# One u tile in eight transposed by TensorE instead of VectorE and DMA, with half of its output product in native fp32, and output copies in pairs

## Chip, cores and metric

The kernel runs on one core of a Trainium2 chip, as one program of 30891 instructions. The metric is the device time in microseconds of one execution. Three runs of the kernel before gave 1365.64, 1365.99 and 1366.42 us; the median is 1365.99 us.

## What is computed

The reference has three parts that follow each other on an array of 8 x 3072 rows with 256 columns: a spectral layer (FFT, complex weights, soft threshold, inverse FFT), a soft mixture of experts with 32 slots, and a feed-forward layer with a normalised softmax. The change touches only the last one, here with N = 24576 rows:

```python
def _moe2_ref(x, w_in, w_out, g_ln):
    h = x @ w_in                                   # N x 1024
    e = np.exp(h - h.max(-1, keepdims=True))
    sm = e / (e.sum(-1, keepdims=True) + 1e-09)
    solu = h * sm
    mu, var = solu.mean(-1), solu.var(-1)
    ln = (solu - mu) / np.sqrt(var + 1e-06) * g_ln
    return ln @ w_out                              # N x 256
```

## The kernel before

Phase 1 (to about 655 us) does the spectral layer and the experts' statistics; phase 2, from there to the end, does all that `_moe2_ref` asks for. Phase 2 works on NI = 192 tiles of 128 rows. The order of its instructions is written out by hand: the loop `for i in range(NI + 6)` at the end of `phase2` calls small functions, each for another tile, and every engine takes its instructions in that order. In iteration i the calls that matter are:

- `hmat(i + 3)`: two TensorE products of 512 columns write h, negated, into a PSUM tile `hps` (pool `ph_p`, 3 buffers). The columns of h stand in the permuted order of `gst`.
- `rowmax(i + 2)`, `umul(i + 1)`, `blocks(i + 1)`: VectorE's three passes of 1024 columns. `umul` multiplies h by its exponential into `u` (SBUF) and is the last reader of `hps`. `blocks` transposes u in blocks of 32 x 32 into `tb`; then four DMAs on SP's queue move the blocks between partitions into `t2` (128 KB each), so that `t2` holds u transposed.
- `store(i - 6)` and `late_c(i)`: further DMAs on SP's queue. An output store of 512 KB goes out every fourth iteration; a reload of the coefficients `ct` (four DMAs of 128 KB) every eighth. Both fall in iterations with i mod 8 = 7.
- `outp(i - 6)`, `vari(i)`, `expo(i + 2)`, `uhi(i - 1)`: ScalarE's passes: output copy from `po` to `osb`, squares for the variance, exponential of h, and the rounding of 768 of the 1024 columns of `t2` to fp32r (`uh`).
- `uhi(i - 1)` and `ulo(i - 1, n)`: on GpSimd the rounding of the other 256 columns and two subtractions that leave the remainder `ul`. `rstd` adds four small instructions every fourth iteration.
- `prod(i - 3)`: 24 fp32r products of 256 columns into `po`: uh by gw_h, uh by gw_l, then ul by gw_h. Two tiles share one PSUM tile `po2` (pool `po_p`, 2 buffers), so that the first product of an even tile waits until both tiles of the pair two back are copied out.

The last two tiles (`direct(i)`) already go another way: TensorE transposes u (`trans`, line 92, with `gstn`, an h in natural column order), and `direct_parts` splits the result.

A few lines that say more than a sentence:

```python
ps = ph_p.tile([128, DFF], F32, name="hps", tag="hps")     # hmat
SP.dma_start(out=t2[:, a, :], in_=t[z].rearrange("i (b x) -> i b x", b=4))   # blocks, a = 0..3
mm(ps, uh[:, f, :], gw[:, f, 0, :], f == 0, False)         # prod, f = 0..7
mm(ps, uh[:, f, :], gw[:, f, 1, :], False, False)
mm(ps, ul[:, f, :], gw[:, f, 0, :], False, f == 7)         # prod, second loop
```

Of the kernel before, what the change touches and what calls it, by code (L numbers as in the profile page):

```python
# [8 lines left out]
F32 = mybir.dt.float32  # L9
F32R = mybir.dt.float32r  # L10
# [3 lines left out]
AF = mybir.ActivationFunctionType  # L14
ALU = mybir.AluOpType
# [20 lines left out]
def kernel(  # L36
# [24 lines left out]
    PE, ACT, DVE, POOL, SP = nc.tensor, nc.scalar, nc.vector, nc.gpsimd, nc.sync  # L61
    B, N, D = x.shape
# [5 lines left out]
    DFF = 1024  # L68
    NI = T // 128
# [775 lines left out]
    def phase2(p2: ExitStack, pw: ExitStack):  # L845
        k_p = p2.enter_context(tc.tile_pool(name="k2_p", bufs=1))
        c_p = p2.enter_context(tc.tile_pool(name="c_p", bufs=1))

        gw = k_p.tile([128, 8, 2, D], F32R, name="gw")
        gw_h, gw_l = gw[:, :, 0, :], gw[:, :, 1, :]  # L850
        gst = k_p.tile([128, DFF], F32R, name="gst")
        gstn = k_p.tile([128, DFF], F32R, name="gstn")
        cts = {}


# [8 lines left out]
        p = ExitStack()  # L864
# [5 lines left out]
        ps = pt.tile([128, 2, 32], F32, name="pslt", tag="pt")  # L870
# [62 lines left out]
        v = psl.rearrange("p d (o s) -> p d o s", o=1).to_broadcast([128, 2, 4, 32])  # L933
# [3 lines left out]
        for fh in range(2):  # L937
            n = 0
# [13 lines left out]
        def right(name, bufs, **k):  # L952
            return p2.enter_context(tc.tile_pool(name=name, bufs=bufs, side="right", **k))

        e_p = right("e_p", 2)
        u_p = right("u_p", 4)
        o_p = right("o_p", 2)
# [3 lines left out]
        po_p = right("po_p", 2, space=PSUM)  # L961
        NG = NI // 4
        ctt, hps, et, ut, uht, stt, osb, pot = {}, {}, {}, {}, {}, {}, {}, {}


        def pieces(j):
            if j >= NG:
                return
            b, r = divmod(j, 6)
            h, ah = divmod(r, 2)  # L970
            src = cts[b, h][:, 16 * ah:16 * ah + 16, :].rearrange("p a j -> p (a j)")
            ctt[j] = src
            if ah:
                c_todo[4 * j + 3] = (b + 1, h)


        def hmat(i):
            if i >= NI:
                return
            j, k = divmod(i, 4)  # L980
            ps = ph_p.tile([128, DFF], F32, name="hps", tag="hps")
            for fh in range(2):
                mm(ps[:, 512 * fh:512 * fh + 512], ctt[j][:, 128 * k:128 * k + 128], (gstn if direct(i) else gst)[:, 512 * fh:512 * fh + 512])
            hps[i] = ps

        def stats(i):
            j, k = divmod(i, 4)
            if k == 0 and j not in stt:
                stt[j] = s_p.tile([128, 6, 4], F32, name="st", tag="st")
            return stt[j], k  # L990

        def rowmax(i):
            if i >= NI:
                return
            st, k = stats(i)
            DVE.tensor_reduce(out=st[:, 0, k:k + 1], in_=hps[i], op=ALU.min, axis=AX.X)  # L996

        def expo(i):
            if i >= NI:
                return  # L1000
            st, k = stats(i)
            e = e_p.tile([128, DFF], F32, name="e", tag="e")
            ACT.activation(out=e, in_=hps[i], func=AF.Exp, bias=st[:, 0, k:k + 1], scale=-1.0, accum_out=st[:, 1, k:k + 1])  # L1003
            et[i] = e

        def umul(i):
            if i >= NI:
                return
            st, k = stats(i)
            u = u_p.tile([128, DFF], F32, name="u", tag="u")  # L1010
            DVE.scalar_tensor_tensor(out=u, in0=hps.pop(i), scalar=1.0, in1=et.pop(i), op0=ALU.mult, op1=ALU.mult, accum_out=st[:, 2, k:k + 1])  # L1011
            ut[i] = u


        def direct(i):
            return i >= NI - 2

        def gst_order():
            POOL.tensor_copy(out=gstn.rearrange("p (c j b) -> p b c j", c=8, b=4), in_=gst.rearrange("p (b c j) -> p b c j", b=4, c=8).bitcast(F32))

        def blocks(i):
            if i >= NI or direct(i):
                return
            t = u_p.tile([128, DFF], F32, name="tb", tag="tb", bufs=3)
            DVE.transpose(out=t, in_=ut[i])  # L1027
            t2 = u_p.tile([128, 4, 256], F32, name="t2", tag="t2", bufs=3)
            for a in range(4):
                z = slice(32 * a, 32 * a + 32)  # L1030
                SP.dma_start(out=t2[:, a, :], in_=t[z].rearrange("i (b x) -> i b x", b=4))  # L1031
            t2t[i] = t2
# [9 lines left out]
        def parts(i):  # L1042
            uh = u_p.tile([128, 8, 128], F32R, name="uh", tag="uh")
            ul = u_p.tile([128, 8, 128], F32R, name="ul", tag="ul")
            uht[i] = (uh, ul)
            return uh, ul
# [9 lines left out]
                DVE.tensor_tensor(out=ul[:, z, :], in0=ps[:, z, :], in1=uh[:, z, :].bitcast(F32), op=ALU.subtract)  # L1056


        HA = 6

        def uhi(i):
            if i < 0 or direct(i):
                return
            uh, ul = parts(i)
            v = t2t[i].rearrange("p a (c j) -> p c a j", c=8)
            w = uh.rearrange("p c (a j) -> p c a j", a=4)
            ACT.activation(out=w[:, 0:HA], in_=v[:, 0:HA], func=AF.Copy)  # L1067
            POOL.tensor_copy(out=w[:, HA:8], in_=v[:, HA:8])  # L1068

        def ulo(i, n):  # L1070
            if i < 0 or direct(i):
                return
            uh, ul = uht[i]
            z = slice(4 * n, 4 * n + 4)
            v = t2t[i].rearrange("p a (c j) -> p c a j", c=8)[:, z]
            w = uh[:, z, :].rearrange("p c (a j) -> p c a j", a=4)
            POOL.tensor_tensor(out=ul[:, z, :].rearrange("p c (a j) -> p c a j", a=4), in0=v, in1=w.bitcast(F32), op=ALU.subtract)  # L1077
            if n:
                t2t.pop(i)


        def vari(i):
            if i >= NI:
                return
            st, k = stats(i)
            sq = e_p.tile([128, DFF], F32, name="sq", tag="sq", bufs=1)
            ACT.activation(out=sq, in_=ut.pop(i), func=AF.Square, bias=st[:, 2, k:k + 1], scale=-float(DFF), accum_out=st[:, 3, k:k + 1])  # L1087

        def prod(i):
            if i < 0 or i >= NI:  # L1090
                return
            uh, ul = uht.pop(i)
            if i % 2 == 0:
                pot[i // 2, 0] = po_p.tile([128, 2, D], F32, name="po2", tag="po2")
            ps = pot[i // 2, 0][:, i % 2, :]
            for f in range(8):
                mm(ps, uh[:, f, :], gw[:, f, 0, :], f == 0, False)
                mm(ps, uh[:, f, :], gw[:, f, 1, :], False, False)
            for f in range(8):
                mm(ps, ul[:, f, :], gw[:, f, 0, :], False, f == 7)  # L1100
            pot[i] = ps


        def rstd(i):
# [9 lines left out]
            POOL.tensor_tensor(out=st[:, 3, k], in0=st[:, 3, k], in1=st[:, 1, k], op=ALU.add)  # L1114
            POOL.tensor_tensor(out=st[:, 4, k], in0=st[:, 3, k], in1=mhalf[:, k], op=ALU.pow)

        o_todo = {}

        def outp(i):
            if i < 0:  # L1120
                return
            j, k = divmod(i, 4)
            b, r = divmod(j, 6)
            h, ah = divmod(r, 2)
            v = out.rearrange("(b h lm a) d -> b h lm a d", b=B, h=3, a=8)[b, h, :, 4 * ah:4 * ah + 4, :]
            if k == 0:
                osb[0] = o_p.tile([128, 4, D], F32, name="osb", tag="osb")
            o = osb[0]
            ACT.activation(out=o[:, k], in_=pot.pop(i), func=AF.Copy, scale=stt[j][:, 4, k:k + 1])  # L1129
            if j == NG - 1:  # L1130

                SP.dma_start(out=v[:, k, :], in_=o[:, k, :])
            elif k == 3:
                o_todo[i + 2] = (v, o)


        def store(i):
# [36 lines left out]
        expo(1)  # L1174
        umul(0)
        blocks(0)
        for i in range(NI + 6):
            j, k = divmod(i, 4)
            hmat(i + 3)
            trans(i)  # L1180
            rowmax(i + 2)
            umul(i + 1)
            blocks(i + 1)
            store(i - 6)
            late_c(i)
            last_c(i)
            outp(i - 6)
            vari(i)
            expo(i + 2)
            direct_parts(i)  # L1190
            if i <= NI:
                uhi(i - 1)
                ulo(i - 1, 0)
            rstd(i)
            if i <= NI:
                ulo(i - 1, 1)
            if i == 40:
                gst_order()
            if k == 1:
                pieces(j + 2)  # L1200
            prod(i - 3)
        while o_todo:
            store(min(o_todo))
# [140 lines left out]
```

## Time and profile before

| | |
|---|---|
| median of three runs | 1365.99 us |
| profiled execution: span from first to last instruction | 1364.4 us (the page gives no other time for it; the median lies 1.6 us above) |
| busy share of the span: PE, DVE, ACT, POOL | 93%, 88%, 76%, 72% |
| phase 2, from tile 50 to tile 191 (836.9 to 1342.4 us): busy us of 505.5 | PE 476.3, DVE 492.8, ACT 472.9, POOL 461.6 |

PE is TensorE, DVE VectorE, ACT ScalarE, POOL GpSimd, and SPq SyncE's queue of DMA issues. The shares over the whole span mix two phases with different limits; the windows of phase 2 are the ones to read. An instruction's recorded duration overlaps that of its successor on the same engine, so the cost of one is read from its start to the next one's start.

### The profile page before, as it was taken

To read this page: it belongs to the slowest core of one execution; us is meant where nothing else is said; L and a number is where in the kernel's file an instruction comes from. 1 tells how busy PE (TensorE), PEld (TensorE's weight loads), DVE (VectorE), ACT (ScalarE), POOL (GpSimd) and SP (SyncE) were. 2 spreads that over 40 slices of the span, in tenths; PEclk is the share of its full clock that TensorE was granted. 3 is DMA by queue.
4 is the path that set the end of the run, shared out by engine and by line. 5 is a ranking of instruction groups with operands and counts; after the bars stand their busy time and mean duration, and the time that the engine had idled before them with its cause. 6 is when DMAs were issued, how large, how long until landed. Compare 5 with 4: busy or idle time off the path is not lost.

```text
span 1364.4 us, 30891 instructions
## 1 busy us (share of the span) xinstructions
PE 1268.9 (93%) x10784; PEld 1126.9 (83%) x10784; DVE 1207.1 (88%) x1691; ACT 1038.8 (76%) x2005; POOL 979.4 (72%) x1045
## 2 busy tenths in 40 slices
PE   6999999999999999878699989999999999899998
PEld 3888888888878788855588888988898889888897
DVE  7787988888888989765999999999999999999994
ACT  5567665666667665533799889999899999899995
POOL 5557575757565654221588989989899999889996
PEclk8899999999999999999799999999999999999999
DMA  8966463646445464168478788778877888787874
GB/s 267 289 202 175 124 193 111 209 117 186 140 144 167 126 181 155 62 223 291 108 179 220 188 210 209 198 197 209 205 194 203 196 198 217 196 206 191 201 197 125
DMA packets 190746, 252.70 MB, mean 185 GB/s; under 512 B 21504, under 2 KB 155392, under 8 KB 190592
## 3 DMA queue, kind: packets, MB, share of 16 engines
q1 hardware_dynamic: 190256, 249.57, 67.3%
q8 instruction: 85, 1.39, 0.4%
q10 hardware_dynamic: 336, 1.18, 0.2%
q14 instruction: 69, 0.57, 0.1%
HBM read 91.94 MB, written 59.11 MB: 111 GB/s over the span
## 4 chain that ended last, share of the span: by engine, by line
PE 37%; POOL 14%; DMA 13%; issue 12%; DVE 10%; SPq 8%; ACT 6%; POOLq 0%; ACTq 0%; DVEq 0%
PE po L89 10%; DMA t<-tb 9%; POOL ul L1077 8%; PE pb L89 6%; PE pm L89 6%; SPq L1031 6%; PE s L89 4%; PE xps L89 4%; PE pa L89 3%; DMA xc<-in_x_dram 3%; POOL x L235 2%; PE sps L92 2%; SPq L861 2%; POOL uh L1068 2%; ACT uh L1067 1%
## 5 line engine op out<-in xcount | busy, mean ns | idle before, releaser
L1077 POOL TENSOR_TENSOR ul<-t,uh 128x512 fp32r<-128x512 f32 x380 | 486.1, 1296 | 31.8 <-ACT uh L1067 30.7
L89 PEld LDWEIGHTS po<-gw,uh 128*128 128x128 f32 x3072 | 384.9, 190 | 80.8 <-ACT osb L1129 72.2
L89 PE MATMUL po<-gw,uh 128*128 128x256 f32 x3072 | 404.9, 284 | 41.7 <-ACT osb L1129 41.4
L346 POOL TENSOR_TENSOR s<-yb,s 128x512 f32<-128x512 f32 x95 | 132.4, 1394 | 216.9 <-DVE s L345 187.8
L1027 DVE STREAM_TRANSPOSE tb<-u 128x1024 f32<-128x1024 f32 x190 | 236.7, 1246 | 7.0 <-DMA t<-tb 0.4
L1011 DVE SCALAR_TENSOR_TENSOR u<-hps,e 128x1024 f32<-128x1024 f32 x192 | 232.3, 1210 | 11.6 <-ACT e L1003 11.1
L996 DVE TENSOR_REDUCE st<-hps 128x1 f32<-128x1024 f32 x192 | 227.7, 1186 | 1.7 <-PE hps L89 1.7
L1087 ACT ACTIVATE sq<-u,st 128x1024 f32<-128x1024 f32 x192 | 221.3, 1152 | 0.2 <-DVE u L1011 0.2
L1003 ACT ACTIVATE e<-hps,st 128x1024 f32<-128x1024 f32 x192 | 214.1, 1115 | 7.2 <-DVE st L996 6.6
L89 PE MATMUL po<-gw,ul 128*128 128x256 f32 x1536 | 213.0, 281 | 0.8 <-POOL ul L1077 0.8
L89 PEld LDWEIGHTS po<-gw,ul 128*128 128x128 f32 x1536 | 195.3, 189 | 1.1 <-POOL ul L1077 1.0
L1067 ACT ACTIVATE uh<-t 128x768 fp32r<-128x768 f32 x190 | 160.5, 845 | 44.6 <-DMA t<-tb 41.1
L235 POOL TENSOR_TENSOR x<-xc,x 96x512 fp32r<-96x512 f32 x120 | 164.7, 1381 | 29.5 <-ACT x L234 28.4
L89 PE MATMUL hps<-gst,ct 128*128 128x512 f32 x380 | 119.5, 397 | 12.0 <-DVE u L1011 10.5
L261 ACT ACTIVATE asb<-s 96x512 f32<-96x512 f32 x112 | 66.6, 595 | 73.8 <-PE s L89 73.2
L89 PE MATMUL s<-x,df_h 96*96 96x512 f32 x240 | 105.0, 440 | 12.9 <-ACT x L234 4.6
L1068 POOL CAST uh<-t 128x256 fp32r<-128x256 f32 x190 | 75.9, 400 | 49.9 <-DMA t<-tb 46.3
L89 PEld LDWEIGHTS xps<-d_sb,apt 128*128 128x128 f32 x768 | 99.4, 194 | 14.1 <-issue 2.9
L89 PE MATMUL xps<-d_sb,apt 128*128 128x128 f32 x768 | 105.8, 281 | 2.1 <-DMA apt<-ad 1.6
L1129 ACT ACTIVATE osb<-po,st 128x256 f32<-128x256 f32 x192 | 89.5, 468 | 10.2 <-PE po L89 9.1
L234 ACT ACTIVATE x<-xc 96x512 fp32r<-96x512 f32 x120 | 75.1, 626 | 13.2 <-DMA xc<-in_x_dram 13.2
L297 DVE TENSOR_TENSOR xsum<-xps,xi 128x256 f32<-128x256 f32 x96 | 39.8, 414 | 47.9 <-ACT xh L296 44.8
(204 smaller groups left out, 2232.1 us busy)
## 6 DMA issues: line engine op xcount, KB each, us to landing
t<-tb SPq DMA_DIRECT2D x760, 128.0 KB, 2.8
apt<-ad SPq DMA_DIRECT2D x96, 256.0 KB, 4.2
out_dram<-osb SPq DMA_DIRECT2D x47, 512.0 KB, 3.7
xc<-in_x_dram SPq DMA_DIRECT2D x56, 384.0 KB, 3.9
ad<-asb SPq DMA_DIRECT2D x56, 384.0 KB, 3.4
ct<-c_dram SPq DMA_DIRECT2D x96, 128.0 KB, 3.9
wt<-in_moe_w_dram SPq DMA_DIRECT2D x21, 512.0 KB, 8.8
ws<-in_moe_w_dram SPq DMA_DIRECT2D x22, 256.0 KB, 5.9
```

Of the source, the lines that this page charges most:

```text
L89: PE.matmul(out=out, lhsT=lhsT, rhs=rhs, start=start, stop=stop)
L235: POOL.tensor_tensor(out=lo, in0=t, in1=hi.bitcast(F32), op=ALU.subtract)
L346: (DVE if last else POOL).tensor_tensor(out=s, in0=y, in1=s, op=ALU.subtract)
L996: DVE.tensor_reduce(out=st[:, 0, k:k + 1], in_=hps[i], op=ALU.min, axis=AX.X)
L1003: ACT.activation(out=e, in_=hps[i], func=AF.Exp, bias=st[:, 0, k:k + 1], scale=-1.0, accum_out=st[:, 1, k:k + 1])
L1011: DVE.scalar_tensor_tensor(out=u, in0=hps.pop(i), scalar=1.0, in1=et.pop(i), op0=ALU.mult, op1=ALU.mult, accum_out=st[:, 2, k:k + 1])
L1027: DVE.transpose(out=t, in_=ut[i])
L1067: ACT.activation(out=w[:, 0:HA], in_=v[:, 0:HA], func=AF.Copy)
L1068: POOL.tensor_copy(out=w[:, HA:8], in_=v[:, HA:8])
L1077: POOL.tensor_tensor(out=ul[:, z, :].rearrange("p c (a j) -> p c a j", a=4), in0=v, in1=w.bitcast(F32), op=ALU.subtract)
L1087: ACT.activation(out=sq, in_=ut.pop(i), func=AF.Square, bias=st[:, 2, k:k + 1], scale=-float(DFF), accum_out=st[:, 3, k:k + 1])
L1129: ACT.activation(out=o[:, k], in_=pot.pop(i), func=AF.Copy, scale=stt[j][:, 4, k:k + 1])
```

## The change

For tiles with i mod 8 = 5 between 16 and 190 (21, 29, ..., 189: 22 tiles, `turned(i)`) VectorE's block transpose and the four DMAs fall away. In iteration i - 1, after 16 of the 24 products of another tile, TensorE transposes u (8 instructions) back into the tile's own `hps` buffer; ScalarE copies all 1024 columns to SBUF (`raw`); GpSimd splits only columns 512 to 1023 into a high and a low part. The tile's output product has 4 products in native fp32 for the first half (with `gwf`, the sum of gw's two parts) and 12 in fp32r for the second. Its h is made with `gstn`. In iteration i the product of tile i - 3 is split around `hmat(i + 3)`, and `expo` goes ahead of `vari`. Output copies are made two at a time in every even iteration; a store now follows its copy by the same two iterations, and so falls in iterations with i mod 4 = 2. `gst_order` moves from i = 40 to i = 8, and four sums make `gwf` in iterations 10 to 16.

```diff
+        f_p = right("f_p", 1)
+        gwf = f_p.tile([128, 8, D], F32, name="gwf")
+        gstn = f_p.tile([128, DFF], F32R, name="gstn")
...
-                mm(ps[:, 512 * fh:512 * fh + 512], ctt[j][:, 128 * k:128 * k + 128], (gstn if direct(i) else gst)[:, 512 * fh:512 * fh + 512])
+                mm(ps[:, 512 * fh:512 * fh + 512], ctt[j][:, 128 * k:128 * k + 128], (gstn if direct(i) or turned(i) else gst)[:, 512 * fh:512 * fh + 512])
...
+        def turned(i):
+            return i % 8 == 5 and 16 < i < NI - 2
...
+        def gw_sum(n):
+            z = slice(2 * n, 2 * n + 2)
+            POOL.tensor_tensor(out=gwf[:, z], in0=gw[:, z, 0].bitcast(F32), in1=gw[:, z, 1].bitcast(F32), op=ALU.add)
+
         def blocks(i):
-            if i >= NI or direct(i):
+            if i >= NI or direct(i) or turned(i):
                 return
...
+        def turn(i):
+            ps = hps.pop(i).rearrange("p (c j) -> p c j", c=8)
+            for c in range(8):
+                tp(ps[:, c, :], ut[i][:, 128 * c:128 * c + 128])
+            raw, hl = parts(i)
+            ACT.activation(out=raw.bitcast(F32), in_=ps, func=AF.Copy)
+
+        def turned_parts(i, n):
+            raw, hl = uht[i]
+            r = raw[:, 4:8].bitcast(F32)
+            if n == 0:
+                POOL.tensor_copy(out=hl[:, 0:4], in_=r)
+            else:
+                POOL.tensor_tensor(out=hl[:, 4:8], in0=r, in1=hl[:, 0:4].bitcast(F32), op=ALU.subtract)
...
-        def prod(i):
+        def prod(i, left=0):
...
+                if turned(i):
+                    ops = [(uh[:, f, :].bitcast(F32), gwf[:, f, :]) for f in range(4)]
+                    hi = [(f, ul[:, f - 4, :], ul[:, f, :]) for f in range(4, 8)]
+                else:
+                    ops = []
+                    hi = [(f, uh[:, f, :], ul[:, f, :]) for f in range(8)]
+                for f, h, _ in hi:
+                    ops += [(h, gw[:, f, 0, :]), (h, gw[:, f, 1, :])]
+                ops += [(l, gw[:, f, 0, :]) for f, _, l in hi]
...
+            ops = pr_ops[i]
+            while len(ops) > left:
+                mm(*ops.pop(0))
...
-                o_todo[i + 2] = (v, o)
+                o_todo[i + 1] = (v, o)
...
-        for i in range(NI + 6):
+        for i in range(NI + 5):
             j, k = divmod(i, 4)
+            if turned(i):
+                prod(i - 3, 12)
             hmat(i + 3)
...
-            outp(i - 6)
-            vari(i)
-            expo(i + 2)
+            if i % 2 == 0:
+                outp(i - 6)
+                outp(i - 5)
+            if turned(i):
+                expo(i + 2)
+                vari(i)
+            else:
+                vari(i)
+                expo(i + 2)
...
-            if i == 40:
+            if i == 8:
                 gst_order()
+            if i in (10, 12, 14, 16):
+                gw_sum(i // 2 - 5)
...
+            if turned(i + 1):
+                prod(i - 3, 8)
+                turn(i + 1)
             prod(i - 3)
```

TensorE before, iteration 20 and the one behind it (`po` is the output product, of tiles 17 and 18, `hps` the h of the tile three ahead):

```order
L89 MATMUL hps<-gst,ct 128x512 x2
L89 MATMUL po_9957<-gw,uh 128x256 x16
L89 MATMUL po_9957<-gw,ul 128x256 x8
L89 MATMUL hps<-gst,ct 128x512 x2
L89 MATMUL po_10057<-gw,uh 128x256 x16
```

TensorE after the change, the same place: iteration 20, iteration 21 and the start of 22. Line 92 is the transposes of tile 21, into its own `hps` buffer:

```order
L89 MATMUL hps<-gst,ct 128x512 x2
L89 MATMUL po_9966<-gw,uh 128x256 x16
L92 MATMUL hps<-ident,u 128x128 x8
L89 MATMUL po_9966<-gw,ul 128x256 x8
L89 MATMUL po_10047<-gw,uh 128x256 x12
L89 MATMUL hps<-gst,ct 128x512 x2
L89 MATMUL po_10047<-gw,uh 128x256 x4
L89 MATMUL po_10047<-gw,ul 128x256 x8
L89 MATMUL hps<-gst,ct 128x512 x2
```

Eight transposes now stand between the 16th and the 17th product of tile 17, and the next h stands behind 8 and 12 products (of tiles 17 and 18) that follow the transposes, where 24 products stood between one h and the next.

ScalarE after the change, iteration 20 to the start of 22 (line 1169 is the output copy, 1118 `vari`, 1005 `expo`, 1094 `uhi`, 1073 the copy of the transposed tile 21):

```order
L1169 ACTIVATE osb<-po_9862,st 128x256 x2
L1118 ACTIVATE sq,st<-u,st 128x1024
L1005 ACTIVATE e,st<-hps,st 128x1024
L1094 ACTIVATE uh<-t_9896 128x768
L1073 ACTIVATE uh<-hps 128x1024
L1005 ACTIVATE e,st<-hps,st 128x1024
L1118 ACTIVATE sq,st<-u,st 128x1024
L1094 ACTIVATE uh<-t_9947 128x768
L1169 ACTIVATE osb<-po_9966,st 128x256 x2
```

Before, each iteration had one output copy, then `vari`, `expo` and `uhi`. Now iteration 20 has two output copies and, behind `uhi`, the copy of tile 21; iteration 21 has none of these and begins with `expo`.

SP's queue before, the blocks of tiles with i mod 8 = 0 to 5 (line 1031), with the store (1140) and the reload of `ct` (861):

```order
L1031 DMA t_11372<-tb 128x1x256 x4
L1140 DMA out_dram<-osb 128x1024
L861 DMA ct<-c_dram 32x1024 x4
L1031 DMA t_11431<-tb 128x1x256 x4
L1031 DMA t_11479<-tb 128x1x256 x4
L1031 DMA t_11529<-tb 128x1x256 x4
L1031 DMA t_11578<-tb 128x1x256 x4
L1140 DMA out_dram<-osb 128x1024
L1031 DMA t_11632<-tb 128x1x256 x4
```

SP's queue after the change, tiles with i mod 8 = 3, 4, 6, 7, 0 and 1 (blocks line 1040, store 1180, reload 860):

```order
L1040 DMA t_11505<-tb 128x1x256 x4
L1180 DMA out_dram<-osb 128x1024
L1040 DMA t_11556<-tb 128x1x256 x4
L1040 DMA t_11674<-tb 128x1x256 x4
L1040 DMA t_11710<-tb 128x1x256 x4
L1180 DMA out_dram<-osb 128x1024
L1040 DMA t_11757<-tb 128x1x256 x4
L860 DMA ct<-c_dram 32x1024 x4
L1040 DMA t_11814<-tb 128x1x256 x4
```

Store and reload now have a tile's blocks between them, and four DMAs are gone between the blocks of tiles 4 and 6.

## Rows read from the trace of the kernel before

**Rows 1.** Windows by stage: busy us (x instructions) of each engine, granted clock, DMA share.
```profile
0.00:655.00 655.00, 614.23 (x5782) 513.59 (x5782) 534.92 (x924) 393.36 (x854) 347.44 (x262) 0.98 0.57 175
836.90:1342.40 505.50, 476.28 (x3663) 446.66 (x3663) 492.82 (x563) 472.91 (x847) 461.58 (x564) 1.00 0.81 201
```

**Rows 2.** Timeline, DVE: `umul` of tiles 2, 26, 50 and 191 (start us, us).
```profile
661.39 1.21 DVE L1011 SCALAR_TENSOR_TENSOR u<-hps,e 128x1024 f32<-128x1024 f32 x1
...
746.24 1.21 DVE L1011 SCALAR_TENSOR_TENSOR u<-hps,e 128x1024 f32<-128x1024 f32 x1
...
836.88 1.21 DVE L1011 SCALAR_TENSOR_TENSOR u<-hps,e 128x1024 f32<-128x1024 f32 x1
...
1342.42 1.23 DVE L1011 SCALAR_TENSOR_TENSOR u<-hps,e 128x1024 f32<-128x1024 f32 x1 [0.88 <-ACT e L1003]
```

**Rows 3.** Timeline, DVE: one tile's three passes and the next tile's first.
```profile
1117.11 1.19 DVE L996 TENSOR_REDUCE st<-hps 128x1 f32<-128x1024 f32 x1
1118.21 1.21 DVE L1011 SCALAR_TENSOR_TENSOR u<-hps,e 128x1024 f32<-128x1024 f32 x1
...
1119.47 1.25 DVE L1027 STREAM_TRANSPOSE tb<-u 128x1024 f32<-128x1024 f32 x1
1120.64 1.19 DVE L996 TENSOR_REDUCE st<-hps 128x1 f32<-128x1024 f32 x1
```

**Rows 4.** Timeline, PE: one iteration from h to h (xcount: that many in a row).
```profile
1121.78 0.63 PE L89 MATMUL hps<-gst,ct 128*128 128x512 f32 x2
1122.24 2.04 PE L89 MATMUL po<-gw,uh 128*128 128x256 f32 x16
1124.12 1.10 PE L89 MATMUL po<-gw,ul 128*128 128x256 f32 x8
1125.06 0.62 PE L89 MATMUL hps<-gst,ct 128*128 128x512 f32 x2
```

**Rows 5.** Timeline, ACT: one iteration from output copy to output copy.
```profile
1118.35 0.46 ACT L1129 ACTIVATE osb<-po,st 128x256 f32<-128x256 f32 x1
...
1119.84 1.10 ACT L1003 ACTIVATE e<-hps,st 128x1024 f32<-128x1024 f32 x1
1120.84 0.19 ACT L1003 ACTIVATION_READ_ACCUMULATOR e<-hps,st 128x1 f32 x1
1120.92 0.84 ACT L1067 ACTIVATE uh<-t 128x768 fp32r<-128x768 f32 x1
1121.66 0.46 ACT L1129 ACTIVATE osb<-po,st 128x256 f32<-128x256 f32 x1
```

**Rows 6.** Timeline, POOL: `rstd`, then one tile's rounding and subtractions.
```profile
715.05 0.19 POOL L1112 TENSOR_SCALAR st<-st 128x4 f32<-128x4 f32 x1
...
716.86 1.29 POOL L1077 TENSOR_TENSOR ul<-t,uh 128x512 fp32r<-128x512 f32 x1
718.09 0.40 POOL L1068 CAST uh<-t 128x256 fp32r<-128x256 f32 x1
718.45 2.55 POOL L1077 TENSOR_TENSOR ul<-t,uh 128x512 fp32r<-128x512 f32 x2
720.95 0.39 POOL L1068 CAST uh<-t 128x256 fp32r<-128x256 f32 x1
```

**Rows 7.** Waits, 700 to 1350 us: who waits for whom (us in total, times, longest).
```profile
PE po L89 <- ACT osb L1129: 40.7, 40, 2.3
ACT uh L1067 <- DMA t<-tb: 40.7, 38, 2.4
...
DVE u L1011 <- ACT e L1003: 10.9, 19, 1.1
```

**Rows 8.** Timeline, ACT: `uhi` behind store and reload, and behind a store alone [idle before].
```profile
1161.33 0.84 ACT L1067 ACTIVATE uh<-t 128x768 fp32r<-128x768 f32 x1 [2.13 <-DMA t<-tb]
...
1176.00 0.84 ACT L1067 ACTIVATE uh<-t 128x768 fp32r<-128x768 f32 x1 [1.27 <-DMA t<-tb]
```

**Rows 9.** Timeline, PE: the transposes of tile 190 and what follows; then their window.
```profile
1343.14 1.03 PE L92 MATMUL pu<-ident,u 128*128 128x128 f32 x8
1343.93 2.15 PE L89 MATMUL po<-gw,uh 128*128 128x256 f32 x16
...
1343.00:1344.00 1.00, 1.00 (x12) 1.00 (x10) 0.65 (x2) 1.00 (x3) 0.84 (x3) 1.00 0.93 192
```

**Rows 10.** Timeline, PE: native fp32 products of 256 columns (two and a half of them).
```profile
603.25 1.24 PE L89 MATMUL pgm<-wo,ones 128*128 128x256 f32 x5
```

**Rows 11.** Lines by form, 700 to 1350 us: busy us, mean ns of one.
```profile
L92 PE MATMUL pu<-ident,u 128*128 128x128 f32 x16 | 2.1, 272 | 0.0
...
L1019 POOL CAST gstn<-gst 128x1024 fp32r<-128x1024 f32 x1 | 2.1, 2059 | 0.0
```

More of the change, by code (lines that the diff above doesn't have):

```diff
@@ L851, in phase2 @@
         gst = k_p.tile([128, DFF], F32R, name="gst")
-        gstn = k_p.tile([128, DFF], F32R, name="gstn")
         cts = {}
@@ L1010, in umul @@
             u = u_p.tile([128, DFF], F32, name="u", tag="u")
-            DVE.scalar_tensor_tensor(out=u, in0=hps.pop(i), scalar=1.0, in1=et.pop(i), op0=ALU.mult, op1=ALU.mult, accum_out=st[:, 2, k:k + 1])
+            DVE.scalar_tensor_tensor(out=u, in0=hps[i] if turned(i) else hps.pop(i), scalar=1.0, in1=et.pop(i), op0=ALU.mult, op1=ALU.mult, accum_out=st[:, 2, k:k + 1])
             ut[i] = u
@@ L1062, in uhi @@
             if i < 0 or direct(i):
+                return
+            if turned(i):
+                turned_parts(i, 0)
                 return
@@ L1071, in ulo @@
             if i < 0 or direct(i):
+                return
+            if turned(i):
+                if n:
+                    turned_parts(i, 1)
                 return
@@ L1087, in vari @@
             ACT.activation(out=sq, in_=ut.pop(i), func=AF.Square, bias=st[:, 2, k:k + 1], scale=-float(DFF), accum_out=st[:, 3, k:k + 1])
-        def prod(i):
+        def prod(i, left=0):
             if i < 0 or i >= NI:
                 return
[L1092 to L1101, printed above, removed]
+            if i not in pr_ops:
+                uh, ul = uht.pop(i)
+                if i % 2 == 0:
+                    pot[i // 2, 0] = po_p.tile([128, 2, D], F32, name="po2", tag="po2")
+                ps = pot[i // 2, 0][:, i % 2, :]
+                if turned(i):
[7 more added lines that the diff above has]
+                ops += [(l, gw[:, f, 0, :]) for f, _, l in hi]
+                pot[i] = ps
+                pr_ops[i] = [(ps, a, b, n == 0, n == len(ops) - 1) for n, (a, b) in enumerate(ops)]
+            ops = pr_ops[i]
+            while len(ops) > left:
+                mm(*ops.pop(0))
         def rstd(i):
@@ L1115, in rstd @@
             POOL.tensor_tensor(out=st[:, 4, k], in0=st[:, 3, k], in1=mhalf[:, k], op=ALU.pow)
-        o_todo = {}
+        o_todo, pr_ops = {}, {}
         def outp(i):
-            if i < 0:
+            if i < 0 or i >= NI:
                 return
@@ L1176, in phase2 @@
         blocks(0)
-        for i in range(NI + 6):
+        for i in range(NI + 5):
             j, k = divmod(i, 4)
+            if turned(i):
+                prod(i - 3, 12)
             hmat(i + 3)
@@ L1186, in phase2 @@
             last_c(i)
-            outp(i - 6)
-            vari(i)
-            expo(i + 2)
+            if i % 2 == 0:
+                outp(i - 6)
+                outp(i - 5)
+            if turned(i):
+                expo(i + 2)
[3 more added lines that the diff above has]
+                expo(i + 2)
             direct_parts(i)
```

## The prediction

> **What bounds the kernel now.** I read the windows by stage first, to see whether one engine fills a stage: phase 1 is not touched by the change, and in phase 2 between tiles 50 and 191 all four engines are busy for 91 to 97% of 505.5 us, VectorE most [rows 1]. With shares so close, busy time does not tell the bound, so I went to the timelines and read each engine's cost of one tile from start to start.
>
> VectorE takes 3.53 us per tile (1117.11 to 1120.64), of which the block transpose is 1.17 (1119.47 to 1120.64) [rows 3]. TensorE takes 3.28 us (1121.78 to 1125.06): h 0.46, 16 products 1.88, 8 products 0.94 [rows 4]. ScalarE takes 3.31 us (1118.35 to 1121.66), with 0.74 for `uhi` [rows 5]. GpSimd takes 2.86 us (718.09 to 720.95), and `rstd` 1.81 more every fourth tile (715.05 to 716.86) [rows 6]. For eight tiles, the period of the change: VectorE 28.3, GpSimd 8 x 2.86 + 2 x 1.81 = 26.5, ScalarE 26.5, TensorE 26.2.
>
> The real pace is read from `umul`, which every tile has once [rows 2]. Tiles 2 to 26 take 84.85 us for 24 tiles, 28.3 for eight: VectorE alone, without a gap. Tiles 26 to 50 take 90.64 us, 30.2 for eight; in this stretch lie the late work on the last `ct` and `gst_order`. Tiles 50 to 191 take 505.54 us for 141 tiles, 28.7 for eight: VectorE's 28.3 and 0.4 of gaps. Where the gaps come from is in the list of waits: VectorE waits for ScalarE's `e` (10.9 us in total), and ScalarE for the block DMAs (40.7 us, 38 times) [rows 7]. The long ones are behind a store with a reload (2.13 us) and behind a store alone (1.27 us) [rows 8]. So VectorE is the bound, and late DMAs cost a little on top of it.
>
> **The change, part by part, for a group of eight tiles.**
>
> *VectorE.* One transpose goes: 28.3 - 1.17 = 27.1 us. Nothing is added.
>
> *TensorE.* Eight transposes are added. The same eight for tile 190 take 0.79 us, start to the next product's start (1343.14 to 1343.93), at a granted clock of 1.00, the 2.4 GHz level [rows 9]. The turned tile's product loses 12 fp32r products of 1.88 / 16 = 0.118 us each, 1.41 us, and gets 4 native ones. No such product stands in phase 2; the nearest rows are those of the mean of `wo`, same shape, recorded as two instructions for one product. Five of them take 1.24 us, and with 0.16 for the last one's tail (1.10 - 0.94 in [rows 4]) that is 0.216 each, 0.43 per product [rows 10]. Four cost 1.73, so 0.32 more. Sum: 26.2 + 0.79 + 0.32 = 27.3 us. TensorE, now 2 us below VectorE, becomes the highest by 0.2. The bounds of the part it adds: 0.79 + 0 if the native products cost no more than those they replace, and 2.18 + 0.32 if the transposes do not overlap each other, for one alone is recorded with 272 ns [rows 11]. I take 1.1, since [rows 9] is this very instruction in this very place, between products.
>
> *ScalarE.* `uhi` (0.74) goes for the turned tile, and a copy of 1024 PSUM columns comes. The nearest row is `expo`, which reads as many from the same PSUM tile: 1.00 us from its start to its accumulator read [rows 5]. So 26.5 + 0.26 = 26.7 us. Making the output copies two at a time adds none.
>
> *GpSimd.* The turned tile has one cast of 512 columns (between twice the 256-column cast, 0.36 x 2, and half of the 1024-column one, 1.03 [rows 6, 11]) and one subtraction (1.27) in place of 2.86: some 0.7 us less in each group, 25.8. Once, in iterations 10 to 16, four sums of 512 columns are added, which I price as the 512-column subtraction, 4 x 1.27 = 5.1 us, and `gst_order` (2.06 us [rows 11]) comes into the same stretch. GpSimd has 28.3 - 26.5 = 1.8 us of room per group there. Up to tile 26 that is 5 us of room for 7.2 us of work, so I charge 2 us; the bounds are 0 and 7.
>
> *SP's queue and the DMAs.* 22 times four DMAs go. Store and reload no longer stand in one iteration: the blocks behind them now follow one store, or one reload, and the store with i mod 8 = 2 is followed by one tile's blocks and then by a gap of four DMAs. ScalarE comes to those blocks (tile 4) late, because iteration 4 holds two output copies and the turned copy: 4.7 us in place of 3.3. I expect the wait behind the lone store to vanish and the other to shrink, but the period shrinks as well, by about 1 us per group, and leaves less time for each transfer. I count no gain here, and keep the 0.4 us of gaps.
>
> *The PE wait for output copies* (40.7 us, 40 times [rows 7]) goes, for the pair that an even tile needs is now copied one iteration earlier. Today it costs nothing, since VectorE ends last; it is needed so that TensorE, with 27.3 us, can run through.
>
> *The new wait.* The h three tiles ahead needs the turned tile's PSUM buffer, so it waits for `umul`, eight transposes and ScalarE's copy. Let T be the end of `umul` of the turned tile. The transposes end at T + 0.8 at the soonest, the copy at T + 1.9 to 2.2. VectorE asks for that h one full iteration later, at T + 3.5, and h takes 0.46: there are 0.9 to 1.2 us of room. On TensorE 0.94 + 1.41 = 2.35 us of products lie between transposes and h, about twice the copy; behind the h wait the rest of that product and everything after it. If the cover fails, each us by which the copy ends after T + 3.0 costs a us of VectorE, once per group.
>
> **Sum.** The new pace is the highest engine, 27.3, with the gaps of today: 27.7 to 27.8 us for eight tiles, 0.95 below 28.7. Tiles 50 to 191: 141 / 8 x 0.95 = 16.7 us. Tiles 26 to 50, three groups: 3 x 0.95 = 2.8 us. Tiles 2 to 26 have one turned tile: 0.95 gained, 2 charged for GpSimd, -1.0. The end is as before: the last `umul` is followed by the same copies and products. Together 18.5 us off the span of 1364.4, so 1345.9; the median of the runs lies 1.6 us above that span, which gives **1347.5 us**. With the upper TensorE bound in place of 0.79 + 0.32 the gain would be near nothing; with no gaps left (27.3) it would be 1.4 per group and, with the excess of tiles 26 to 50 gone too, some 30 us.
>
> **Rivals.**
>
> *Transposes that do not overlap.* If each of the eight waits for its own weights and its own drain, they cost 8 x 0.272 = 2.18 us [rows 11], TensorE needs 28.7 us per group and is the bound at today's pace: 1366 us, or 1373 us if the 0.4 us of gaps come on top. Against it: 0.79 us for eight [rows 9]. Chance 4%. The Trainium skill (TensorE: Matmul & The Clock Gate, Part 4) gives about 275 ns for a transpose in a kernel and says that transposes do not count as activity for the clock gate. By its figure eight cost 2.2 us, and this change would gain nothing; in [rows 9] the eight took 0.79 us and the granted clock of that stretch stayed at 1.00, so here the trace speaks against both halves of that rule.
>
> *ScalarE and DMA hold the pace.* ScalarE's 26.7 us plus today's DMA waits of 40.7 us over some 180 tiles, 1.8 per group, is 28.5 us. For: the waits of [rows 8] are as long as two transposes. Against: a part of them is room that ScalarE only has because VectorE is slower, and store and reload are now apart. Half-way, at 28.2 to 28.4, the gain is 0.4 per group, 8 us, less 1: 1359 us. Chance 13%.
>
> *The copy comes late (slower).* ScalarE's copy stands behind two output copies, `vari`, `expo` and `uhi`, and that `uhi` can wait 2.13 us for its blocks [rows 8]. If it did so in each group, with ScalarE already 1 us behind, the copy would end near T + 5.3, VectorE would lose 2.3 us where it saves 1.17, and 22 groups would add 25 us: 1391 us. It decides for slower from a copy that ends after T + 4.2. Against: the blocks that this `uhi` needs (tile 3) are issued ahead of the store, not behind it. Chance 8%.
>
> *The change does not do what it says.* The order shows the transposes, the native products (4 with `gwf`) and 22 block transposes fewer. What it does not show is whether the native products run as two passes; if as one, TensorE needs 26.2 + 0.79 - 0.55 = 26.4 and VectorE's 27.1 is the bound: 0.2 per group better, 1344 us. Chance 3%.
>
> **How the numbers follow.** The forecast has 72%. Its own range is 27.3 to 28.1 us per group, 1336 to 1354 us. The range to hold the time 8 times in 10 reaches on to the half-way case: 1336 to 1360 us; left out are the copy that comes late, transposes that do not overlap, and a little at each end. A measurement of this kernel tells about 0.2%, 2.7 us, from no change. Faster by more: 72 + 3 and most of 13, 85%. Within: the no-gain end of two rivals, 6%. Slower: 9%.
>
> **What would show it.** VectorE with 22 transposes fewer and `umul` to `umul` 2.36 us apart once in eight; the eight transposes in 0.8 us at a granted clock of 1.00; the native products at 0.43 us; the copy about 1.0 us; the PE wait for output copies near zero; eight tiles in 27.7 us behind tile 50. I am wrong if PE waits for line 1073 by over 1 us in a group, if VectorE's `rowmax` waits for h, if ScalarE's DMA waits grow, or if tiles 8 to 26 lose more than 2 us to GpSimd.

## The result and the profile after

The change takes 1346.39 us (median of four runs, 1345.94 to 1346.88) against 1366.2 us before, the median of four with a fourth run of 1368.51: the quotient of the two medians is 0.9855. The ratio on record, which the percentages below go by, is 0.9839, 95% interval 0.9822 to 0.9856. The forecast was 1347.5 us, with a range of 1336 to 1360. The span of the profiled execution fell from 1364.4 to 1344.4 us, by 20.0 where 18.5 had been forecast. The number came out right; two terms behind it did not, and they cancelled, so that it came out within 1.1 us is in part luck.

First the windows of the changed kernel, with the columns of [rows 1], for tiles 50 to 191:

```profile
835.50:1322.60 487.10, 485.54 (x3728) 467.65 (x3727) 471.70 (x545) 473.44 (x844) 443.45 (x545) 1.00 0.74 189
```

TensorE is now busy for 485.54 of 487.10 us, VectorE for 471.70, which is 97%; in [rows 1] it was 476.3 and 492.8 of 505.5. TensorE is the fuller engine, as forecast, and its records show next to no gap, where the forecast had kept 0.4 us in each group. Records of TensorE run past the start of the next one, so a short wait can hide in them; one of 0.1 us is read below.

The timeline of VectorE, `umul` of tiles 2, 26, 50 and 191, answers to [rows 2]:

```profile
661.69 1.21 DVE L1013 SCALAR_TENSOR_TENSOR u<-hps,e 128x1024 f32<-128x1024 f32 x1
...
748.63 1.21 DVE L1013 SCALAR_TENSOR_TENSOR u<-hps,e 128x1024 f32<-128x1024 f32 x1
...
835.49 1.21 DVE L1013 SCALAR_TENSOR_TENSOR u<-hps,e 128x1024 f32<-128x1024 f32 x1
...
1322.61 1.22 DVE L1013 SCALAR_TENSOR_TENSOR u<-hps,e 128x1024 f32<-128x1024 f32 x1 [1.11 <-ACT e L1005]
```

| stretch | before, us | after, us | forecast change | measured change |
|---|---|---|---|---|
| tiles 2 to 26 | 84.85 | 86.94 | +1.0 | +2.1 |
| tiles 26 to 50 | 90.64 | 86.86 | -2.8 | -3.8 |
| tiles 50 to 191 | 505.54 | 487.12 | -16.7 | -18.4 |

The rest, -0.2 on the tail and +0.3 ahead of tile 2, makes the 20.0. Behind tile 50 eight tiles take 27.6 us in place of 28.7.

One group of that stretch, the timeline of TensorE (start us, us), from one h to the h of the same place eight tiles on:

```profile
1029.39 0.62 PE L89 MATMUL hps<-gst,ct 128*128 128x512 f32 x2
...
1039.71 2.04 PE L89 MATMUL po<-gw,uh 128*128 128x256 f32 x16
1041.69 1.09 PE L92 MATMUL hps<-ident,u 128*128 128x128 f32 x8
1042.53 1.18 PE L89 MATMUL po<-gw,ul 128*128 128x256 f32 x8
1043.55 1.57 PE L89 MATMUL po<-gw,uh 128*128 128x256 f32 x12
1044.96 0.63 PE L89 MATMUL hps<-gst,ct 128*128 128x512 f32 x2
...
1053.88 1.89 PE L89 MATMUL po<-gwf,uh 128*128 128x256 f32 x8
1055.42 1.78 PE L89 MATMUL po<-gw,ul 128*128 128x256 f32 x12
1057.04 0.62 PE L89 MATMUL hps<-gst,ct 128*128 128x512 f32 x2
```

From 1029.39 to 1057.04 are 27.65 us, and no row shows idle time. The eight transposes take 0.84 us (0.79 in [rows 9]), at a granted clock of 1.00 in that window, the 2.4 GHz level; the turned tile's product 3.16 us (1053.88 to 1057.04), against 3.14 forecast.

The same place on VectorE and ScalarE, with `umul` of the turned tile first (the READ rows are VectorE's accumulator reads, line 1073 the copy of the transposed tile):

```profile
1040.41 1.21 DVE L1013 SCALAR_TENSOR_TENSOR u<-hps,e 128x1024 f32<-128x1024 f32 x1
1041.55 0.08 DVE L1013 DVE_READ_ACCUMULATOR u<-hps,e 128x1 f32 x1
1041.55 1.22 DVE L998 TENSOR_REDUCE st<-hps 128x1 f32<-128x1024 f32 x1
...
1045.70 1.22 DVE L998 TENSOR_REDUCE st<-hps 128x1 f32<-128x1024 f32 x1 [0.51 <-PE hps L89]
```

```profile
1043.01 1.01 ACT L1073 ACTIVATE uh<-hps 128x1024 f32<-128x1024 f32 x1
1043.91 1.10 ACT L1005 ACTIVATE e<-hps,st 128x1024 f32<-128x1024 f32 x1
```

`umul` ends at 1041.63; the transposes start at 1041.69, and the products ahead of them had stretched to 1.98 us from 1.88: TensorE stands at the transposes and waits for u for 0.1 us. The copy is done at about 1043.9, 2.3 us after `umul`, and h starts only at 1044.96, because 20 products stand before it. So `rowmax` waits 0.51 us for h; such a wait stands 14 times in the list below, which covers 22 groups. Two streams close a loop here: VectorE from that `rowmax` to the next turned tile's `umul` end, 27.65 - 4.07 = 23.58 us without a gap, then TensorE from there over transposes, 20 products and h to `rowmax`, 4.07 us (1041.63 to 1045.70).

The list of waits, 700 to 1330 us, answers to [rows 7]:

```profile
ACT uh L1094 <- DMA t<-tb: 19.4, 27, 2.0
DVE u L1013 <- ACT e L1005: 12.1, 17, 1.3
DVE st L998 <- PE hps L89: 7.2, 14, 0.5
```

ScalarE's waits for the block DMAs are half of what they were (40.7), the PE wait for output copies (40.7) has left the list, and the new one is `rowmax` for h.

### The profile page after: what moved, and what is told of

Same layout as the page of the kernel before. It is cut to its first block, busy times and chain, and to the rows that moved or that the text cites. A ratio compares the mean times of both kernels' runs of the same rounds, so it can differ in the third digit from the quotient of the medians.

```text
span 1344.4 us, 30699 instructions
## 1 busy us (share of the span) xinstructions
PE 1282.3 (95%) x10872; PEld 1153.7 (86%) x10872; DVE 1181.0 (88%) x1669; ACT 1042.1 (78%) x2005; POOL 962.1 (72%) x1027
## 4 chain that ended last, share of the span: by engine, by line
PE 51%; DVE 14%; DMA 10%; issue 7%; POOL 7%; SPq 6%; ACT 4%; DVEq 0%; POOLq 0%; ACTq 0%
PE po L89 19%; PE pb L89 7%; PE pm L89 6%; DMA t<-tb 5%; SPq L1040 5%; PE s L89 4%; PE xps L89 4%; POOL ul L1108 3%; PE pa L89 3%; PE hps L89 3%; DMA xc<-in_x_dram 3%; DVE u L1013 3%; DVE tb L1036 2%; PE sps L92 2%; DVE st L998 2%
## 5 line engine op out<-in xcount | busy, mean ns | idle before, releaser
L1108 POOL TENSOR_TENSOR ul<-t,uh 128x512 fp32r<-128x512 f32 x336 | 431.1, 1301 | 32.4 <-ACT uh L1094 30.4
L89 PEld LDWEIGHTS po<-gw,uh 128*128 128x128 f32 x2720 | 346.9, 189 | 14.1
L89 PE MATMUL po<-gw,uh 128*128 128x256 f32 x2720 | 352.8, 281 | 0.0
L89 PE MATMUL po<-gw,ul 128*128 128x256 f32 x1624 | 230.7, 285 | 3.7 <-POOL ul L1108 3.4
L1036 DVE STREAM_TRANSPOSE tb<-u 128x1024 f32<-128x1024 f32 x168 | 209.3, 1246 | 5.8
L89 PEld LDWEIGHTS po<-gw,ul 128*128 128x128 f32 x1624 | 207.0, 188 | 6.2 <-POOL ul L1108 4.9
L1094 ACT ACTIVATE uh<-t 128x768 fp32r<-128x768 f32 x168 | 143.7, 856 | 23.4 <-DMA t<-tb 20.2
L89 PE MATMUL hps<-gst,ct 128*128 128x512 f32 x336 | 106.9, 401 | 12.7 <-DVE u L1013 10.9
L1095 POOL CAST uh<-t 128x256 fp32r<-128x256 f32 x168 | 67.9, 404 | 43.5 <-DMA t<-tb 42.1
L1169 ACT ACTIVATE osb<-po,st 128x256 f32<-128x256 f32 x192 | 81.0, 483 | 7.8 <-PE po L89 7.8
```

## Experiments

Each run is told as its ratio to the kernel before on the same chip, with the 95% interval, and as the pace of eight tiles behind tile 50, worked out from `umul` of tile 50 to that of tile 191 (141 tiles). An edit starts from the changed kernel where its first line names no other.

### Which part brings how much: pairs, store, turned tiles

**pairs_only**

```diff
 def turned(i):
-    return i % 8 == 5 and 16 < i < NI - 2
+    return False
...
-            if i == 8:
+            if i == 40:
                 gst_order()
-            if i in (10, 12, 14, 16):
-                gw_sum(i // 2 - 5)
```

> Only the output copies in pairs and the store that moves with them; no tile is turned, no sums. Theory A (the gain is VectorE's missing transposes; VectorE was the bound, TensorE is now): VectorE still has 28.3 us per eight tiles, only the 0.4 us of gaps behind tile 50 and part of the excess before it can go, 1357 to 1366 us. Rival P (the pairs and the moved store bring most of it, by the 40.7 us of TensorE waits for output copies and the DMA waits): 1346 to 1353 us.

Measured: 1357.02 us, 0.991 (0.9889 to 0.993). The two rows of `umul` of tiles 50 and 191:

```profile
833.45 1.22 DVE L1013 SCALAR_TENSOR_TENSOR u<-hps,e 128x1024 f32<-128x1024 f32 x1
...
1329.78 1.23 DVE L1013 SCALAR_TENSOR_TENSOR u<-hps,e 128x1024 f32<-128x1024 f32 x1
```

496.33 us for 141 tiles, 28.2 for eight: every gap is gone, and VectorE runs at its own 28.3 (the last tiles, without a transpose, make it a little less). The time is at the edge of theory A's range. Its gain of 11 us is more than the 7 us (141 / 8 x 0.4) that I had thought the gaps to be worth: with no tile turned, about half of the change's gain is there, 0.9% of 1.6%. The next two runs part the pairs from the store.

**pairs_old_store**

```diff
 # on top of pairs_only
-                o_todo[i + 1] = (v, o)
+                o_todo[i + 2] = (v, o)
```

> Output copies in pairs alone: no tile turned, and the store two iterations later than in the change, where it stands ahead of the reload of ct as in the kernel before. Theory S (the 0.4 us of gaps per eight tiles, and 11 us of the gain, come from store and reload standing in one iteration): the gaps stay, 28.6 to 28.7 us per eight tiles behind tile 50, 0.997 to 1.000 of the time before. Theory W (they come from TensorE waiting for output copies): the gaps go, 28.3 us, 0.990 to 0.993.

Measured: 1362.7 us, 0.9966 (0.9951 to 0.9982), 28.5 us per eight tiles, both a little below what theory S named: the gaps stay for the most part. ScalarE's wait for blocks behind a store with a reload is still there, in its timeline:

```profile
1104.37 0.84 ACT L1094 ACTIVATE uh<-t 128x768 fp32r<-128x768 f32 x1 [2.79 <-DMA t<-tb]
```

**store_only**

```diff
 # on top of pairs_only
-            if i % 2 == 0:
-                outp(i - 6)
-                outp(i - 5)
+            outp(i - 6)
...
-        for i in range(NI + 5):
+        for i in range(NI + 6):
```

> The other half: one output copy per iteration as before, no tile turned, but the store one iteration sooner, away from the reload. Theory S: 28.3 us per eight tiles behind tile 50, 0.990 to 0.993 of the time before. Theory W: 28.6 to 28.7 us, 0.997 to 1.000.

Measured: 1357.99 us, 0.9929 (0.9909 to 0.9949), 28.2 us per eight tiles. In its list of waits, 836 to 1320 us, TensorE still waits for output copies, and it does no harm: no row of VectorE stands in that list with more than 1.1 us in all.

```profile
PE po L89 <- ACT osb L1169: 19.4, 26, 1.8
ACT uh L1094 <- DMA t<-tb: 18.1, 25, 1.5
```

So theory S holds. The gaps of [rows 2] behind tile 50 come from a store of 512 KB and a reload of four times 128 KB that stand in one iteration ahead of the blocks of the next tile; one iteration between them removes them, with output copies made singly. The edit moves the lone store too, and no run parts the two stores; in the trace before, of 8.2 us that VectorE loses between tiles 50 and 185, 5.9 us lie at the `umul` that follows ScalarE's wait behind store and reload (tiles with i mod 8 = 5), and 1.6 us at the one that follows its wait behind the lone store (i mod 8 = 1). The pairs by themselves are worth 0.3%, a little more than I expected of them.

### What the pairs are for

**no_pairs**

```diff
-                o_todo[i + 1] = (v, o)
+                o_todo[i + 2] = (v, o)
...
-        for i in range(NI + 5):
+        for i in range(NI + 6):
...
-            if i % 2 == 0:
-                outp(i - 6)
-                outp(i - 5)
+            outp(i - 6)
```

> The change with one output copy per iteration and the store where it was. Theory A: TensorE has no idle time left in a group, so waits for output copies (27.3 us between tiles 50 and 191 in the kernel before, hidden there) now show for a third or more: 1353 to 1366 us. Rival Q (these waits stay hidden, as they were in the kernel before): 1345 to 1349 us.

Measured: 1390.86 us, 1.0157 (1.0132 to 1.0182): slower than the kernel before, far outside of both ranges; 29.7 us per eight tiles. The place is the turned tile's, on TensorE, ScalarE and VectorE:

```profile
1035.61 1.03 PE L92 MATMUL hps<-ident,u 128*128 128x128 f32 x8
1036.40 1.19 PE L89 MATMUL po<-gw,ul 128*128 128x256 f32 x8
1038.17 1.70 PE L89 MATMUL po<-gw,uh 128*128 128x256 f32 x12 [0.58 <-ACT osb L1169]
1039.70 0.62 PE L89 MATMUL hps<-gst,ct 128*128 128x512 f32 x2
```

```profile
1036.73 1.03 ACT L1073 ACTIVATE uh<-hps 128x1024 f32<-128x1024 f32 x1 [0.17 <-POOL st L1155]
1037.65 0.47 ACT L1169 ACTIVATE osb<-po,st 128x256 f32<-128x256 f32 x1
```

```profile
1040.43 1.23 DVE L998 TENSOR_REDUCE st<-hps 128x1 f32<-128x1024 f32 x1 [2.07 <-PE hps L89]
```

The 12 products that now stand ahead of h are those of an even tile, which needs the PSUM pair that this iteration's single output copy frees. That copy stands on ScalarE behind the copy of the turned tile. So h waits for line 1073, line 1169 and 12 products in a row, and `rowmax` 2.07 us for h, in each group of that stretch: the list of waits, 836 to 1320 us, has it with 33.3 us, 19 times, three of them short. The store is back beside the reload here too, so this run does not part the two as wholes; but of the 2.1 us that a group behind tile 50 loses against the change, 1.6 lie at this `rowmax`, and 0.5 at a `umul` that waits for ScalarE's `e`. That TensorE's waits were hidden before said nothing of what they cost once its order holds h behind them.

### What sets the new pace

**split8**

```diff
             if turned(i):
-                prod(i - 3, 12)
+                prod(i - 3, 16)
```

> In the turned iteration 8 products of the split tile stand ahead of the next h, in place of 12, so h comes 0.47 us earlier. Theory L (a loop of VectorE's stream and the stretch from umul over the transposes to h sets the 27.65 us per eight tiles; rowmax waits 0.51 us for h): the 0.5 us wait goes, TensorE's own 27.5 us is left, 0.1 us less per group, 1343 to 1346 us. Rival C (ScalarE's copy is what h waits for): h cannot start earlier, TensorE waits for the copy in place of doing products, 1347 to 1355 us.

Measured: 1342.87 us, 0.9813 (0.9791 to 0.9835), 27.5 us per eight tiles: just below theory L's range, with 0.2 us less per group where 0.1 was expected. TensorE behind the transposes, whose u ended at 1039.66, and the wait in the list, 700 to 1330 us:

```profile
1040.59 1.18 PE L89 MATMUL po<-gw,ul 128*128 128x256 f32 x8
1041.62 1.10 PE L89 MATMUL po<-gw,uh 128*128 128x256 f32 x8
1042.56 0.63 PE L89 MATMUL hps<-gst,ct 128*128 128x512 f32 x2
```

```profile
DVE st L998 <- PE hps L89: 0.8, 3, 0.3
```

h comes 2.9 us after u, where it came 3.3 us after it, and the waits of `rowmax` fall from 7.2 us to 0.8. Theory L holds: h may come sooner, and rival C is out. **turn_last** goes at the same loop from its other end:

```diff
             if turned(i + 1):
-                prod(i - 3, 8)
+                prod(i - 3)
                 turn(i + 1)
```

> The eight transposes behind all 24 products of the other tile instead of between the 16th and the 17th. Theory L (loop of umul, transposes, products, h): TensorE has the same work up to h, the copy now starts 0.9 us later and ends about where h begins, so h is late by 0 to 0.5 us, 27.6 to 28.1 us per eight tiles, 1345 to 1353 us. Rival I (the place inside the product is what hides the copy, and 12 products alone do not cover it): TensorE waits for the copy over 0.5 us in each group, 1355 to 1365 us.

Measured: 1341.83 us, 0.9813 (0.9792 to 0.9834), 27.5 us per eight tiles: better than the change, where I expected the same or worse. TensorE at the turned tile:

```profile
1042.48 1.04 PE L92 MATMUL hps<-ident,u 128*128 128x128 f32 x8
1043.27 1.68 PE L89 MATMUL po<-gw,uh 128*128 128x256 f32 x12
1044.79 0.62 PE L89 MATMUL hps<-gst,ct 128*128 128x512 f32 x2
```

u was ready at about 1042.0 (`umul` starts at 1040.75), so the transposes wait for nothing, and the loop from `umul` to h has 12 products in it, not 20. The 12 still cover the copy (1043.60 to 1044.5). I had taken TensorE's order up to h as given and asked when the copy would end; but in the change TensorE comes to the transposes 0.1 us before u is there, and each product between transposes and h makes the loop longer. Moved ahead of the transposes, the eight products fill that wait and leave the loop. Behind the transposes they cost time in this program; they do not save any.

**native_all**

```diff
-            if n == 0:
-                POOL.tensor_copy(out=hl[:, 0:4], in_=r)
-            else:
-                POOL.tensor_tensor(out=hl[:, 4:8], in0=r, in1=hl[:, 0:4].bitcast(F32), op=ALU.subtract)
+            return
...
-                    ops = [(uh[:, f, :].bitcast(F32), gwf[:, f, :]) for f in range(4)]
-                    hi = [(f, ul[:, f - 4, :], ul[:, f, :]) for f in range(4, 8)]
+                    ops = [(uh[:, f, :].bitcast(F32), gwf[:, f, :]) for f in range(8)]
+                    hi = []
```

> All eight blocks of a turned tile's product in native fp32, none in fp32r; GpSimd then has no part of a turned tile. Theory A (TensorE's stream is the bound at 27.65 us): four more native products at 0.385 us in place of 12 at 0.118 add 0.1 us to a group, 0 to 0.2, 1346 to 1350 us less some 2 us for GpSimd's relief up to tile 50. Rival H (GpSimd's splitting is what the half product in native fp32 is there to relieve, and it still limits): 1338 to 1343 us.

Measured: 1346.96 us, 0.9848 (0.9828 to 0.9869), 27.7 us per eight tiles; most groups stand at 27.83, where the change has 27.65. The whole product is recorded as 16 instructions, with the next h and the product behind it:

```profile
1081.67 3.61 PE L89 MATMUL po<-gwf,uh 128*128 128x256 f32 x16
1084.93 0.82 PE L89 MATMUL hps<-gst,ct 128*128 128x512 f32 x2
1085.59 2.06 PE L89 MATMUL po<-gw,uh 128*128 128x256 f32 x16
```

The 16 start 0.216 us apart, and h starts 3.26 us behind the first of them; but that h then takes 0.66 us to the next row (1084.93 to 1085.59), where 0.46 is usual. So 0.20 us of the product fall on the row of h. The product costs 3.46 us, 0.43 for each native one, which is the price of the prediction; the 0.385 of the expectation above had left out the same rest. TensorE has 0.30 us more to do in a group (3.46 for 3.16), and the pace rose by 0.18: the transposes wait for u no longer, and take 0.79 us (1069.53 to 1070.32), so a part of the 0.30 went into time in which TensorE had waited. Rival H is out: GpSimd had nothing to do for a turned tile, and no time came back behind tile 50. Ahead of it some did: tiles 26 to 50 take 85.06 us, 86.86 in the change.

### Ahead of tile 50

**early_sums**

```diff
+        for n in range(4):
+            gw_sum(n)
+        gst_order()
         for i in range(NI + 5):
...
-            if i == 8:
-                gst_order()
-            if i in (10, 12, 14, 16):
-                gw_sum(i // 2 - 5)
```

> The four sums and gst_order ahead of the loop, where GpSimd waits 37 us for the first blocks. Theory G (GpSimd's 7.3 us in iterations 8 to 16 are what tiles 18 to 26 lose, 2.7 us over the pace behind tile 50): 1342.5 to 1344.5 us. Rival D (the loss is from DMAs and the late work on the last ct): 1345.5 to 1347 us.

Measured: 1342.79 us, 0.9813 (0.9793 to 0.9833). Tiles 2 to 26 take 84.46 us in place of 86.94, all of it in tiles 18 to 26. Theory G.

To hold these small gains against the change itself, it ran once more beside their combinations, the same file with no edit, as **after_again**.

> The change itself once more, beside the variants on the same chip. All theories: 0.982 to 0.986 of the time before; with 1368.4 us before on this chip, 1344 to 1349 us. What split8, turn_last and early_sums gained (1342 to 1343 us) counts only against this number: if it comes out at 1343 too, none of the three is a gain.

Measured: 1345.94 us, 0.9838 (0.9819 to 0.9856), 27.6 us per eight tiles. By the pace or the stretch named above the three gains are 3.1 us (split8), 3.3 us (turn_last, which ran on another chip) and 2.5 us (early_sums); by the medians they are 3 to 4 us. The intervals of the ratios overlap, so each rests on its pace or stretch.

**last_early**: the edits of turn_last and early_sums together.

> Transposes behind all 24 products of the other tile, and the sums ahead of the loop. Theory L (both gains are of different stretches, the loop behind tile 50 and GpSimd's backlog up to tile 26): they add, 3.4 us and 2.5 us, 1339 to 1342 us where the change has 1346. Rival N (both only shift the same wait): 1342 to 1344 us.

Measured: 1340.76 us, 0.9796 (0.978 to 0.9813); 27.4 us per eight tiles and 84.24 us for tiles 2 to 26. Each stretch keeps its gain, so they add.

**last_early_cl**

```diff
 # on top of last_early
-            elif i == 33:
+            elif i == 36:
                 SP.dma_start(out=d[0], in_=cl[1].bitcast(F32))
+            elif i == 44:
                 SP.dma_start(out=d[1], in_=cl[0].bitcast(F32))
```

> As last_early, and the two 384 KB stores of the last ct, both in iteration 33 before, one each in iterations 36 and 44, where a turned tile leaves SP's queue without block DMAs. Theory S (DMAs behind each other make the waits): tiles 34 to 42 lose 3 us less, 1336 to 1339 us. Rival R (that loss is GpSimd's, from the last ct's subtractions): as last_early, within 1 us.

Measured: 1337.0 us, 0.9773 (0.9757 to 0.9789). Tiles 34 to 42 take 29.04 us in place of 30.79, tiles 42 to 50 27.36 in place of 27.68. That is 2.1 us of the 3.8 between the medians, and less than the 3 us of theory S, but rival R as it stands, within 1 us, is out. GpSimd has a share in this stretch all the same: native_all, which takes its work off the turned tiles and leaves these stores where they were, needs 28.50 us for tiles 34 to 42, the change 31.02. No run parts the two further. This is the fastest kernel of the study, below both the kernel before and the change.

**last_early_10**

```diff
 # on top of last_early
-            return i % 8 == 5 and 16 < i < NI - 2
+            return i % 10 == 5 and 16 < i < NI - 2
```

> As last_early with one tile in ten turned (i mod 10 = 5). For ten tiles VectorE needs 34.2 us and TensorE 32.8 + 1.4 = 34.2: 27.35 us per eight. Theory E (engine sums alone set the pace): 27.35 in place of 27.45, 1337 to 1341 us. Theory S (the place of stores and reload against the gaps in SP's queue matters): with period 10 against 4 and 8 they meet again in some groups, 27.5 to 27.8 us, 1341 to 1346 us.

Measured: 1341.18 us, 0.981 (0.9789 to 0.9831), 27.5 us per eight tiles. The period is now ten tiles. From tile 50 on, six of 14 stretches of ten take 34.2 us, as the engines' sums alone gave (27.35 for eight); the others take up to 35.3. That fits theory S, but no row shown here tells which transfers meet in them. The time itself cannot be told from last_early's.

## Why the prediction was right

*The bound.* VectorE was the bound, and a group without one transpose is faster until TensorE ends last. That step held: TensorE's busy share went to 99.7%, and native_all, with 0.30 us more to do there in a group, raised the pace by 0.18. What sets the 27.65 us of the change is the loop between VectorE and TensorE, up to 0.2 us above TensorE's own sum: split8 and turn_last, which shorten the loop alone, stand at 27.5.

*The gaps.* This is the first step that failed: "I count no gain here, and keep the 0.4 us of gaps". They went to nothing, and not through the turned tiles: store_only, which moves only the store, brings 0.7% of the 1.6%. I had written that store and reload "no longer stand in one iteration" and seen that the long waits of [rows 8] stood behind both; what I lacked was to take these waits out of the sum for that alone. They were also 0.5 us, not 0.4: the 28.7 that I read up to tile 191 has the last tiles without a transpose in it, and up to tile 186 the pace before was 28.8.

*TensorE's sum.* This is the second: 27.3 us were forecast, 27.65 measured. The transposes (0.84 for 0.79) and the product (3.16 for 3.14) were nearly right. What was missing is 0.1 us of waiting for u, which is the loop; 0.08 us at the restart of the products behind the transposes (1042.53 to 1043.55 is 1.02 us for eight), which stays in split8 and so is TensorE's own; and 0.03 us in each of two iterations. The pace of 27.7 to 27.8 had some 0.35 us too little on TensorE and 0.4 too many gaps in it: two errors of nearly one size with opposite signs.

*The new wait.* I had put the copy's end at T + 1.9 to 2.2 and the room at T + 3.0. The copy ended at T + 2.3, within the room, but h came at T + 3.3 for its place in TensorE's order, and `rowmax` waited 0.51 us. The room was counted against ScalarE, when it was TensorE's own queue that used it.

*GpSimd.* 2 us were charged for sums and `gst_order`; with the 0.6 us that the one turned tile there should have brought, the loss of 2.1 us makes it 2.7. early_sums gets 2.5 of them back, so this was the cause. With the wait of `rowmax`, it is one of two things that I had named as signs of being wrong and that came: tiles 8 to 26 lose 2.1 us, and `rowmax` waits for h. Both errors were small beside the gain.

*The pairs.* "Today it costs nothing" was right: store_only has 19.4 us of that wait and no gap. That it "is needed so that TensorE, with 27.3 us, can run through" was right and far too mild: without the pairs, and with the store back beside the reload, the change is 1.6% slower than the kernel before, and most of what it loses is the wait for h.

*The rivals.* The late copy, 8% and priced at 1391 us, did not come, but its twin is one edit away: no_pairs stands at 1390.86 us, by a chain that I had not drawn, the output copy behind the turned copy; that the two times agree is chance. Transposes that do not overlap are excluded by 0.84 us for eight. The figure of the Trainium skill (TensorE: Matmul & The Clock Gate, Part 4), about 275 ns for one, is close to what a single one is recorded with here (279 ns in the change), and says little of what eight cost in a stream; the clock stayed at 1.00. "Against both halves of that rule" went too far: the transposes stand among products in every group, so no run here shows what the clock does under transposes alone. The native products are recorded as two instructions each, 0.216 us apart, as priced.

## What to carry to other kernels

Here a store of 512 KB and a reload of four times 128 KB in one iteration of one queue cost up to 0.7% more than the same two an iteration apart; look for such a pair in the queue's order before any engine is relieved. When an engine changes from the second to the first in load, look again at each wait that it had hidden, at what now stands in its order behind that wait, and at what it does just before an input that it arrives too early for: eight products moved from behind that input to ahead of it took 0.2 us off each group here. A sum of engine loads gives the pace only if no loop between two engines is longer, so follow one buffer around once and add up both halves.

## What was not expected of the hardware

TensorE was recorded as busy for 99.7% of 487 us, with a granted clock of 1.00, through transposes, fp32r and native fp32 products in turn. The last native fp32 product of a run leaves 0.20 us of its cost on the row behind it, so a run of eight reads as 3.26 us and costs 3.46. ScalarE's copy of 1024 columns out of PSUM (1.02 us recorded, 0.90 from start to start, 1043.01 to 1043.91) was cheaper than the `expo` of the same size that I had priced it by (1.00).
